# Head and tail of a fused S5 state-space and SwiGLU kernel: another order of the first four token tiles, and a last tile stored in three blocks

## The chip, the cores and the metric

The kernel runs on one core of a Trainium2 chip. The core has five engines with instruction streams of their own: TensorE (PE in the profile; its weight loads are PEld), VectorE (DVE), ScalarE (ACT), GpSimd (POOL) and SyncE (SP), which here only issues transfers. They meet through semaphores. Matmul results land in PSUM, 8 banks of 128 x 512 fp32; everything else is in SBUF. The metric is the time of one execution on the device, in microseconds, as the median of several runs.

## The reference

Input `x` is 2048 tokens of 512 features, bf16. It is normalised per token, and the normalised `xn` goes through two branches whose results are added to `x`:

```python
xn = (x - mean) / sqrt(var + 1e-5)
# A: diagonal complex state space, 512 states
Lam_bar = exp(exp(log_dt) * Lam)
Bu  = xn @ (((Lam_bar - 1) / Lam)[:, None] * B).T
h_t = Lam_bar * h_{t-1} + Bu_t
yA  = 2 * Re(h @ C.T) + xn * Dskip
# B: SwiGLU, hidden size 1376
yB  = (silu(xn @ w_gate) * (xn @ w_up)) @ w_down
out = x + yA + yB
```

## The kernel before

The 2048 tokens are 16 token tiles of 128 (`n`), four to a chunk of 512 (`c`). The hidden size is 11 feature tiles of 128 (`fi`), the last of 96. For a chunk and a feature tile TensorE makes gate and up (`gu_mm`, 4 matmuls each over the 512 features in four parts `k`) into two PSUM banks; ScalarE takes both out (Silu and copy), VectorE multiplies them. The B projection (`bproj_tile`) works likewise; VectorE rotates, scans and rotates back (`ssm_ops`). At the end of a chunk `out_ffn` and `out_ssm` add 11 + 8 matmuls per token tile into one bank.

Order is written out by hand: the kernel is under a manual schedule, so each engine executes its instructions as the Python program issues them. Long VectorE work stands in a backlog that `pump` lets out in step with the matmuls; none of it starts before the head ends. PSUM is a pool of 8 banks (`bank()`).

The **head** is the part up to the first 512-column matmul. `x` tiles 0 to 3 and the weights of feature tiles 0 to 3 come in first, over the queues of SP and ScalarE. Each of the four token tiles passes through
- `ln_stats` (VectorE: statistics, then an aggregate),
- `ln_rstd` (VectorE adds epsilon into `ve`, GpSimd raises it to -0.5),
- `norm_dve` (VectorE),
- `xT_pe` (four TensorE transposes into one bank, then one copy of 512 columns to `xnT`, by ScalarE, for tile 3 by VectorE).

Then `head_mm(fi, i)` runs gate and up of the first three feature tiles for that token tile alone: 8 matmuls of 128 columns into the banks `held`. Up to the first transposes TensorE runs dummy matmuls on a tile of zeros (`dummy`), and after them 11 short ones. The state-space parameters are transposed on TensorE too (`prm_transpose`, 12 columns), between token tiles 2 and 3, and go through ScalarE's Exp before its table for Silu is loaded. The order of the calls is:

```python
dummy(11, CW)
ln_stats(0); ln_rstd(0, 1); ln_stats(1); norm_dve(0); ln_rstd(1, 2)
xT_pe(0); dummy(11, 128)
ln_stats(2); norm_dve(1); ln_rstd(2, 3)
head_mm(0, 0); xT_pe(1); head_mm(1, 0); head_mm(2, 0)
```

The **tail** is the last token tile, 15. `out_blocks` cuts its 512 output columns in two blocks of 256; each has its own bank and matmuls, a VectorE addition of the residual and a store, the first on ScalarE's queue and the last on SP's.

Of the kernel before, what the change touches and what calls it, by code (L numbers as in the profile page):

```python
# [23 lines left out]
def kernel(  # L24
# [17 lines left out]
    nc = tc.nc  # L42
    _, L, D = A_x.shape
# [18 lines left out]
    EPS = 1e-5  # L62

    const = ctx.enter_context(tc.tile_pool(name="const", bufs=1))
# [8 lines left out]
    def bank(shape=(128, CW), dtype=F32):  # L73
        return psum.tile(list(shape), dtype, name="ps")
# [48 lines left out]
    prm_rows = const.tile([3 * NQ, 128], BF16, name="prm_rows")  # L123
# [28 lines left out]
    nc.vector.memset(junk[:], 0.0)  # L152
    neg_half = const.tile([128, TPC], F32, name="neg_half")
    nc.vector.memset(neg_half[:], -0.5)
    magic_t = const.tile([128, 1], F32, name="magic_t")
    nc.vector.memset(magic_t[:], MAGIC)
    ident = const.tile([128, 128], BF16, name="ident")
    make_identity(nc, ident[:])
    jidx = const.tile([128, CW], F32, name="jidx")
# [10 lines left out]
    def xn_tile(c):  # L170
        return xn_end if c == NCH - 1 else xall[:, c * TPC:(c + 1) * TPC, :]

    def ln_stats(n):
        nc.vector.bn_stats(out=stats[:, n, :], in_=xall[:, n, :])  # L174
        nc.vector.bn_aggr(out=mv[:, n, :], in_=stats[:, n, :])  # L175

    def ln_rstd(a, b):
        nc.vector.tensor_scalar(out=ve[:, a:b], in0=mv[:, a:b, 1], scalar1=EPS, scalar2=None, op0=ALU.add)  # L178
        nc.gpsimd.tensor_tensor(out=rstd[:, a:b], in0=ve[:, a:b], in1=neg_half[:, 0:b - a], op=ALU.pow)  # L179
# [5 lines left out]
    def norm_dve(n):  # L185
        c, i = divmod(n, TPC)
        nc.vector.tensor_scalar(out=xn_tile(c)[:, i, :], in0=xall[:, n, :], scalar1=mv[:, n, 0:1],  # L187
                                scalar2=rstd[:, n:n + 1], op0=ALU.subtract, op1=ALU.mult)
# [3 lines left out]
        nc.scalar.activation(out=xn_tile(c)[:, i, :], in_=xall[:, n, :], func=ACT.Identity,  # L192
                             scale=rstd[:, n:n + 1], bias=nb[:, n:n + 1])

    def xT_pe(n, on_dve=False):
        c, i = divmod(n, TPC)
        tp = bank((128, KD, 128), BF16)
        for k in range(KD):
            nc.tensor.transpose(out=tp[:, k, :], in_=xn_tile(c)[:, i, k * 128:(k + 1) * 128], identity=ident[:])  # L199
        if on_dve:  # L200
            nc.vector.tensor_copy(out=xnT[:, :, n * 128:(n + 1) * 128], in_=tp[:])
        else:
            nc.scalar.copy(out=xnT[:, :, n * 128:(n + 1) * 128], in_=tp[:])  # L203

    def xT_dma(n):
        c, i = divmod(n, TPC)
# [3 lines left out]
    prm = const.tile([128, 3, NQ], F32, name="prm")  # L210
# [8 lines left out]
    kk, fs1, fc1 = sm("kk", 2, NQ), sm("fs1", 2, NQ), sm("fc1", 2, NQ)  # L219
    V = nc.vector  # L220

    def prm_transpose():
        pp = bank((128, 3 * NQ), BF16)
        nc.tensor.transpose(out=pp[:], in_=prm_rows[:], identity=ident[0:3 * NQ, 0:3 * NQ])  # L224
        return pp

    def params_a(pp):
        V.tensor_copy(out=prm[:].rearrange("p t q -> p (t q)"), in_=pp[:])
        nc.scalar.activation(out=dt_t[:], in_=ldt, func=ACT.Exp)

    def params_a2():
        V.tensor_tensor(out=dre[:], in0=dt_t[:], in1=lre, op=ALU.mult)
        nc.scalar.activation(out=r_t[:], in_=dre[:], func=ACT.Exp)
        nc.scalar.preload_act_table_set("silu_and_others")
        V.scalar_tensor_tensor(out=ws2[:, 0, :], in0=dt_t[:], scalar=INV_2PI, in1=lim, op0=ALU.mult, op1=ALU.mult)
# [168 lines left out]
    def gu_mm(ps, groups, c, fi, lo, hi):  # L404
        fs = fsz[fi]
        for k in range(KD):
            nc.tensor.matmul(ps[:fs, lo:hi], lhsT=wslice(groups, fi, k),  # L407
                             rhs=xnT[:, k, c * CW + lo:c * CW + hi], start=(k == 0), stop=(k == KD - 1))
# [66 lines left out]

    def out_blocks(n):

        return ((0, D // 2), (D // 2, D)) if n == NT - 1 else ((0, D),)

    def out_ffn(n):  # L480
        c, i = divmod(n, TPC)
# [64 lines left out]

    GU = 8 * 0.2163
    BP = 4 * 0.2163
    warm = bank()

    def dummy(n, cols):
        for _ in range(n):
            nc.tensor.matmul(warm[:, 0:cols], lhsT=junk[:, 0:128], rhs=junk[:, 0:cols], start=True, stop=True)
# [15 lines left out]

    H = 3
    held = []

    def head_mm(fi, i):
        if len(held) <= fi:
            held.append((bank(), bank()))
        gu_mm(held[fi][0], wg_g, 0, fi, i * 128, (i + 1) * 128)
        gu_mm(held[fi][1], wu_g, 0, fi, i * 128, (i + 1) * 128)

    dummy(11, CW)
    ln_stats(0)
    ln_rstd(0, 1)
    ln_stats(1)
    norm_dve(0)
    ln_rstd(1, 2)
    xT_pe(0)
    dummy(11, 128)
    ln_stats(2)
    norm_dve(1)  # L590
    ln_rstd(2, 3)
    head_mm(0, 0)
    xT_pe(1)
    head_mm(1, 0)
    head_mm(2, 0)
    ln_stats(3)
    ln_rstd(3, 4)
    norm_dve(2)
    nc.gpsimd.iota(out=jidx[:], pattern=[[1, CW]], base=0, channel_multiplier=0,
                   allow_small_or_imprecise_dtypes=True)  # L600
    head_mm(0, 1)
    xT_pe(2)
    pp = prm_transpose()
    params_a(pp)
    head_mm(1, 1)
    head_mm(2, 1)
    norm_dve(3)
    params_a2()
    head_mm(0, 2)
    xT_pe(3, on_dve=True)  # L610
    head_mm(1, 2)
    head_mm(2, 2)
    params_sin()
    tables = table_ops()
    stats1, norm1 = ln_rest(1, False)
# [2 lines left out]
    queue("ln1", norm1)  # L618
    queue("tables", tables[2:])
    for fi in range(H):  # L620
        head_mm(fi, 3)
        gu_out(0, fi, *held[fi])
        pump(GU / 4)
    pump(2.0)
# [39 lines left out]
    G0 = 7  # L664
    for fi in range(H, G0):
        gateup_tile(0, fi)
# [77 lines left out]
```

## Time and profile before

| | us |
|---|---|
| median of 3 runs (lowest to highest) | 181.16 (181.07 to 181.38) |
| the profiled execution | 181.06 |
| its span, first to last instruction | 179.3 |
| TensorE busy | 174.4 (97%) |
| VectorE busy | 152.8 (85%) |
| ScalarE busy | 93.4 (52%) |
| GpSimd busy | 25.5 (14%) |

Times in the profile count from the start of the span. In a timeline row stand start, length, engine, line, operation, output and inputs, shapes and count; a bracket names the idle time before it and what ended that. A row with a count covers several instructions, from the start of the first to the end of the last. Groups by line give busy time and mean length in ns of one, then the idle time before them. DMA rows give the size and the time from issue to landing. Ends of matmuls are modelled, so a matmul's row is longer than the step to the next one.

### The profile page before, as it was taken

To read this page: it belongs to the slowest core of one execution; us is meant where nothing else is said; L and a number is where in the kernel's file an instruction comes from. 1 tells how busy PE (TensorE), PEld (TensorE's weight loads), DVE (VectorE), ACT (ScalarE), POOL (GpSimd) and SP (SyncE) were. 2 spreads that over 40 slices of the span, in tenths; PEclk is the share of its full clock that TensorE was granted. 3 is DMA by queue.
4 is the path that set the end of the run, shared out by engine and by line. 5 is a ranking of instruction groups with operands and counts; after the bars stand their busy time and mean duration, and the time that the engine had idled before them with its cause. 6 is when DMAs were issued, how large, how long until landed. Compare 5 with 4: busy or idle time off the path is not lost.

```text
span 179.3 us, 2445 instructions
## 1 busy us (share of the span) xinstructions
PE 174.4 (97%) x914; PEld 83.4 (47%) x914; DVE 152.8 (85%) x232; ACT 93.4 (52%) x165; POOL 25.5 (14%) x33
## 2 busy tenths in 40 slices
PE   7899999999999999999999999999999999999993
PEld 2694444444444444444444444444444444444642
DVE  2869997999999999999999999999999999940032
ACT  2279786988499867023998661024866610220000
POOL 5513000000500000028100000013405000150000
DMA  5999656994237500022920000007386900072011
GB/s 165 325 246 242 105 111 194 349 153 98 46 62 183 230 0 0 0 20 18 141 59 2 0 0 4 0 0 76 32 126 88 150 0 0 2 85 36 0 59 59
DMA packets 29371, 15.53 MB, mean 87 GB/s; under 512 B 18064, under 2 KB 29296, under 8 KB 29328
## 3 DMA queue, kind: packets, MB, share of 16 engines
q1 hardware_dynamic: 24416, 11.24, 27.2%
q0 software_dynamic: 3456, 3.28, 14.2%
q10 hardware_dynamic: 1488, 0.85, 1.6%
q8 instruction: 7, 0.11, 0.3%
q14 instruction: 4, 0.03, 0.0%
HBM read 8.03 MB, written 5.24 MB: 74 GB/s over the span
## 4 chain that ended last, share of the span: by engine, by line
PE 95%; DMA 1%; DVE 1%; ACT 0%; issue 0%
PE ps L407 39%; PE ps L487 21%; PE ps L496 15%; PE ps L332 15%; PE ps L433 2%; DMA xall<-in_A_x_dram 1%; PE ps L443 1%; DVE stats L174 1%; PE ps L199 1%; ACT xnT L203 0%; DVE res L499 0%; DVE mv L175 0%; DVE xall L187 0%; DVE ve L178 0%; PE ps L224 0%
## 5 line engine op out<-in xcount | busy, mean ns | idle before, releaser
L407 PE MATMUL ps<-xnT,wg 128*128 128x512 bf16 (+1 forms) x196 | 42.6, 340 | 0.1
L407 PE MATMUL ps<-xnT,wu 128*128 128x512 bf16 (+1 forms) x196 | 42.6, 340 | 0.0
L487 PE MATMUL ps<-wd_sb,guT 128*128 128x512 bf16 (+3 forms) x187 | 38.7, 366 | 0.0
L374 DVE TENSOR_TENSOR_SCAN g<-r_t,car,u 128x512 bf16<-128x512 f32 x24 | 28.9, 1267 | 0.0
L496 PE MATMUL ps<-CF,wt 128*128 128x512 bf16 (+1 forms) x136 | 28.3, 366 | 0.0
L332 PE MATMUL ps<-xnT,BT 128*128 128x512 bf16 x128 | 28.3, 379 | 0.0
L487 PEld LDWEIGHTS <-guT 128*128 128x128 bf16 (+1 forms) x187 | 18.3, 98 | 20.0
L502 ACT CAST res<-ps 128x512 bf16<-128x512 f32 x12 | 7.0, 585 | 38.6 <-PE ps L496 38.6
L421 ACT ACTIVATE guT<-ps 128x512 bf16<-128x512 f32 x40 | 24.7, 618 | 4.1 <-PE ps L407 4.0
L422 ACT CAST u<-ps 128x512 bf16<-128x512 f32 x40 | 24.1, 603 | 4.3 <-PE ps L407 4.0
L407 PEld LDWEIGHTS <-wu 128*128 128x128 bf16 x196 | 17.6, 98 | 17.5
L407 PEld LDWEIGHTS <-wg 128*128 128x128 bf16 x196 | 17.5, 98 | 17.8 <-issue 1.0
L503 POOL DMA_DIRECT2D out_dram<-res x12 | 11.1, 999 | 87.8 <-ACT res L502 87.8
L496 PEld LDWEIGHTS <-wt 128*128 128x128 bf16 x136 | 13.3, 98 | 14.4
L332 PEld LDWEIGHTS <-BT 128*128 128x128 bf16 x128 | 12.5, 98 | 15.1
L334 ACT CAST u<-ps 128x512 bf16<-128x512 f32 x32 | 17.6, 588 | 3.1 <-PE ps L332 3.1
L499 DVE TENSOR_TENSOR res<-ps,xn_end 128x512 bf16<-128x512 f32 (+1 forms) x5 | 2.9, 585 | 14.9 <-PE ps L496 14.9
L426 DVE TENSOR_TENSOR guT<-guT,u 128x1024 bf16<-128x1024 bf16 x20 | 13.5, 681 | 0.0
L179 POOL TENSOR_TENSOR rstd<-ve,neg_half 128x1 f32<-128x1 f32 (+1 forms) x7 | 7.6, 1082 | 39.0 <-DVE ve L178 39.0
L174 DVE BATCH_NORM_STATS2 stats<-xall 128x6 f32<-128x512 bf16 x16 | 10.8, 672 | 2.6 <-DMA xall<-in_A_x_dram 2.6
L342 DVE TENSOR_TENSOR pm<-u,c 128x2048 bf16<-128x2048 bf16 x8 | 9.8, 1221 | 1.2 <-ACT c L259 1.1
L342 DVE TENSOR_TENSOR pm<-g,c 128x2048 bf16<-128x2048 bf16 x8 | 9.8, 1219 | 0.1
(93 smaller groups left out, 141.4 us busy)
## 6 DMA issues: line engine op xcount, KB each, us to landing
out_dram<-in_A_x_dram SPq DMA_DIRECT2D x1, 1536.0 KB, 6.9
out_dram<-res POOLq DMA_DIRECT2D x12, 128.0 KB, 3.2
out_dram<-xall POOLq DMA_DIRECT2D x3, 512.0 KB, 6.4
wd_sb<-in_B_w_down_dram SPq DMA_DIRECT2D x1, 1280.0 KB, 11.1
xall<-in_A_x_dram SPq DMA_DIRECT2D x1, 1024.0 KB, 6.5
wg<-in_B_w_gate_dram SPq DMA_DIRECT2D x2, 384.0 KB, 5.6
wu<-in_B_w_up_dram SPq DMA_DIRECT2D x2, 384.0 KB, 5.3
wu<-in_B_w_up_dram ACTq DMA_DIRECT2D x2, 256.0 KB, 5.1
```

Source lines behind the costliest of these rows:

```text
L174: nc.vector.bn_stats(out=stats[:, n, :], in_=xall[:, n, :])
L332: nc.tensor.matmul(ps[:], lhsT=BT[:, part, k, q * 128:(q + 1) * 128], rhs=xnT[:, k, c * CW:(c + 1) * CW], start=(k == 0), stop=(k == KD - 1))
L334: nc.scalar.copy(out=u_tiles[c][:, part, q, :], in_=ps[:])
L342: V.tensor_tensor(out=t[:], in0=flat(src()[:, i]), in1=flat(tab[:]), op=ALU.mult)
L374: V.tensor_tensor_scan(out=g()[:, part, q, :], data0=r_t[:, q:q + 1].to_broadcast([128, CW]), data1=u_tiles[c][:, part, q, :], initial=ini ...
L407: nc.tensor.matmul(ps[:fs, lo:hi], lhsT=wslice(groups, fi, k), rhs=xnT[:, k, c * CW + lo:c * CW + hi], start=(k == 0), stop=(k == KD - 1))
L421: nc.scalar.activation(out=guT[:fs, fi, :], in_=psg[:fs], func=ACT.Silu)
L422: nc.scalar.copy(out=u_pair[c][:fs, fi % 2, :], in_=psu[:fs])
L426: products.append(lambda: V.tensor_tensor(out=g, in0=g, in1=u, op=ALU.mult))
L487: nc.tensor.matmul(o[:], lhsT=gu_tiles[c][:fsz[fi], fi, i * 128:(i + 1) * 128], rhs=wd_sb[:fsz[fi], fi, lo:hi], start=(fi == 0), stop=False)
L496: nc.tensor.matmul(o[:], lhsT=w_tiles[c][:, part, q, i * 128:(i + 1) * 128], rhs=CF[:, part, q, lo:hi], start=False, stop=(part == 1 and q ...
L503: nc.gpsimd.dma_start(out=out_v[:, n, lo:hi], in_=res[:, lo:hi], accum_op=ALU.add)
```

## The change

In the head:
- ScalarE makes the `rstd` of token tile 0 (`rstd_act`: Ln with epsilon as bias, then Exp with scale -0.5) from a table set that holds both and is loaded ahead; tiles 1 to 3 keep `ln_rstd`.
- `xT_pe` puts two transposes into a bank and copies 256 columns, twice for a token tile; `head_mm` can run over half of `k`, and for tile 0 and tile 1 the first half's matmuls of two feature tiles stand ahead of the second half's.
- VectorE's order: tile 0 is normalised ahead of tile 1's aggregate, tile 1 ahead of tile 2's statistics, tile 2 between tile 3's statistics and its aggregate, tile 3 ahead of the parameters' copy.
- Feature tile 2 runs for token tiles 0 and 1 at once, with 256 columns, after tile 1's other matmuls.
- The parameter transpose shares a bank with token tile 2's second half.
- There are 10 wide dummies and 6 short ones.

In the tail the last token tile has blocks of 256, 128 and 128 columns, the first two stored from ScalarE's queue and the last from SP's.

```diff
-    magic_t = const.tile([128, 1], F32, name="magic_t")
-    nc.vector.memset(magic_t[:], MAGIC)
+    eps_t = const.tile([128, 1], F32, name="eps_t")
+    nc.vector.memset(eps_t[:], EPS)
...
+    def rstd_act(n):
+
+        nc.scalar.activation(out=ve[:, n:n + 1], in_=mv[:, n, 1:2], func=ACT.Ln, bias=eps_t[:, 0:1])
+        nc.scalar.activation(out=rstd[:, n:n + 1], in_=ve[:, n:n + 1], func=ACT.Exp, scale=-0.5)
...
-    def xT_pe(n, on_dve=False):
+    def xT_pe(n, parts, on_dve=False, prm_too=False):
+
         c, i = divmod(n, TPC)
-        tp = bank((128, KD, 128), BF16)
-        for k in range(KD):
-            nc.tensor.transpose(out=tp[:, k, :], in_=xn_tile(c)[:, i, k * 128:(k + 1) * 128], identity=ident[:])
-        if on_dve:
-            nc.vector.tensor_copy(out=xnT[:, :, n * 128:(n + 1) * 128], in_=tp[:])
-        else:
-            nc.scalar.copy(out=xnT[:, :, n * 128:(n + 1) * 128], in_=tp[:])
+        kp = KD // parts
+        for k0 in range(0, KD, kp):
+            tp = bank((128, kp * 128 + 3 * NQ), BF16)
+            for k in range(k0, k0 + kp):
+                nc.tensor.transpose(out=tp[:, (k - k0) * 128:(k - k0 + 1) * 128],
+                                    in_=xn_tile(c)[:, i, k * 128:(k + 1) * 128], identity=ident[:])
+            if prm_too and k0 + kp == KD:
+                prm_transpose(tp[:, kp * 128:])
+            dst, src = xnT[:, k0:k0 + kp, n * 128:(n + 1) * 128], tp[:, 0:kp * 128].rearrange("p (k t) -> p k t", k=kp)
+            if on_dve:
+                nc.vector.tensor_copy(out=dst, in_=src)
+            else:
+                nc.scalar.copy(out=dst, in_=src)
+        return tp[:, kp * 128:]
...
-        return ((0, D // 2), (D // 2, D)) if n == NT - 1 else ((0, D),)
+        return ((0, D // 2), (D // 2, D - 128), (D - 128, D)) if n == NT - 1 else ((0, D),)
...
-    warm = bank()
+    H = 3
+    held = [(bank(), bank()) for _ in range(H)]
+    warm = held[0][0]
...
+    def head_mm(which, lo, hi, ks, fis):
+
+        for fi in fis:
+            for k in ks:
+                nc.tensor.matmul(held[fi][which][:, lo * 128:hi * 128], lhsT=wslice((wg_g, wu_g)[which], fi, k),
+                                 rhs=xnT[:, k, lo * 128:hi * 128], start=(k == 0), stop=(k == KD - 1))
+
+    allk = range(KD)
+    nc.scalar.preload_act_table_set("natural_log_exp_and_others")
+    dummy(10, CW)
     ln_stats(0)
-    ln_rstd(0, 1)
-    ln_stats(1)
+    rstd_act(0)
+    nc.vector.bn_stats(out=stats[:, 1, :], in_=xall[:, 1, :])
     norm_dve(0)
+    nc.vector.bn_aggr(out=mv[:, 1, :], in_=stats[:, 1, :])
     ln_rstd(1, 2)
-    xT_pe(0)
-    dummy(11, 128)
+    xT_pe(0, 2)
+    dummy(6, 128)
+    norm_dve(1)
     ln_stats(2)
-    norm_dve(1)
     ln_rstd(2, 3)
-    head_mm(0, 0)
-    xT_pe(1)
-    head_mm(1, 0)
-    head_mm(2, 0)
-    ln_stats(3)
+
+    head_mm(0, 0, 1, range(0, HK), (0, 1))
+    head_mm(0, 0, 1, range(HK, KD), (0, 1))
+    head_mm(1, 0, 1, allk, (0,))
+    xT_pe(1, 2)
+    head_mm(1, 0, 1, allk, (1,))
+    nc.vector.bn_stats(out=stats[:, 3, :], in_=xall[:, 3, :])
+    norm_dve(2)
+    nc.vector.bn_aggr(out=mv[:, 3, :], in_=stats[:, 3, :])
     ln_rstd(3, 4)
-    norm_dve(2)
...
-    head_mm(0, 1)
-    xT_pe(2)
-    pp = prm_transpose()
-    params_a(pp)
-    head_mm(1, 1)
-    head_mm(2, 1)
-    norm_dve(3)
+    head_mm(0, 1, 2, range(0, HK), (0, 1))
+    head_mm(0, 1, 2, range(HK, KD), (0, 1))
+    head_mm(1, 1, 2, allk, (0, 1))
+    head_mm(0, 0, 2, allk, (2,))
+    pp = xT_pe(2, 2, prm_too=True)
+    head_mm(1, 0, 2, allk, (2,))
+    norm_dve(3)
+    params_a(pp)
     params_a2()
-    head_mm(0, 2)
-    xT_pe(3, on_dve=True)
-    head_mm(1, 2)
-    head_mm(2, 2)
+    head_mm(0, 2, 3, range(0, HK), range(H))
+    head_mm(0, 2, 3, range(HK, KD), range(H))
+    head_mm(1, 2, 3, allk, (0,))
+    xT_pe(3, 2, on_dve=True)
+    head_mm(1, 2, 3, allk, (1, 2))
...
     for fi in range(H):
-        head_mm(fi, 3)
+        head_mm(0, 3, 4, allk, (fi,))
+        head_mm(1, 3, 4, allk, (fi,))
         gu_out(0, fi, *held[fi])
```

More of the change, by code (lines that the diff above doesn't have):

```diff
@@ L220, with prm_transpose @@
     V = nc.vector
[L222 to L225, printed above, removed]
+    def prm_transpose(pp):
+        nc.tensor.transpose(out=pp, in_=prm_rows[:], identity=ident[0:3 * NQ, 0:3 * NQ])
     def params_a(pp):
-        V.tensor_copy(out=prm[:].rearrange("p t q -> p (t q)"), in_=pp[:])
+        V.tensor_copy(out=prm[:].rearrange("p t q -> p (t q)"), in_=pp)
         nc.scalar.activation(out=dt_t[:], in_=ldt, func=ACT.Exp)
@@ L568, in ln_rest @@
         return ops, tail
[L572 to L581, printed above, removed]
+    HK = KD // 2
+    def head_mm(which, lo, hi, ks, fis):
[6 more added lines that the diff above has]
+    dummy(10, CW)
     ln_stats(0)
-    ln_rstd(0, 1)
-    ln_stats(1)
+    rstd_act(0)
+    nc.vector.bn_stats(out=stats[:, 1, :], in_=xall[:, 1, :])
     norm_dve(0)
+    nc.vector.bn_aggr(out=mv[:, 1, :], in_=stats[:, 1, :])
     ln_rstd(1, 2)
-    xT_pe(0)
-    dummy(11, 128)
+    xT_pe(0, 2)
+    dummy(6, 128)
+    norm_dve(1)
     ln_stats(2)
-    norm_dve(1)
     ln_rstd(2, 3)
-    head_mm(0, 0)
-    xT_pe(1)
-    head_mm(1, 0)
-    head_mm(2, 0)
-    ln_stats(3)
+    head_mm(0, 0, 1, range(0, HK), (0, 1))
[6 more added lines that the diff above has]
+    nc.vector.bn_aggr(out=mv[:, 3, :], in_=stats[:, 3, :])
     ln_rstd(3, 4)
-    norm_dve(2)
     nc.gpsimd.iota(out=jidx[:], pattern=[[1, CW]], base=0, channel_multiplier=0,
                    allow_small_or_imprecise_dtypes=True)
-    head_mm(0, 1)
-    xT_pe(2)
-    pp = prm_transpose()
+    head_mm(0, 1, 2, range(0, HK), (0, 1))
[5 more added lines that the diff above has]
+    norm_dve(3)
     params_a(pp)
-    head_mm(1, 1)
-    head_mm(2, 1)
-    norm_dve(3)
     params_a2()
-    head_mm(0, 2)
-    xT_pe(3, on_dve=True)
-    head_mm(1, 2)
-    head_mm(2, 2)
+    head_mm(0, 2, 3, range(0, HK), range(H))
[3 more added lines that the diff above has]
+    head_mm(1, 2, 3, allk, (1, 2))
     params_sin()
```

## The prediction

> **What bounds the kernel now.** I read the page first, its busy times and its chain of waits, then the timeline of each engine for the first 14 us and the last 5 us, which are the only places that the change touches.
>
> ```profile
> PE 174.4 (97%) x914; PEld 83.4 (47%) x914; DVE 152.8 (85%) x232; ACT 93.4 (52%) x165; POOL 25.5 (14%) x33
> ...
> PE 95%; DMA 1%; DVE 1%; ACT 0%; issue 0%
> ```
>
> TensorE is the bound: 95% of the chain. What is left is the time before its first useful matmul, a few stalls among the short matmuls of the head, and the tail behind its last one. The change can win or lose only there. TensorE, head and start of the wide matmuls:
>
> ```profile
> 1.20 3.95 PE L553 MATMUL ps<-junk 128*128 128x512 bf16 x11 [1.20 <-DVE magic_t L156]
> ...
> 5.72 0.40 PE L199 MATMUL ps<-ident,xall 128*128 128x128 bf16 x4 [0.58 <-DVE ve L178]
> 5.96 0.78 PE L553 MATMUL ps<-junk 128*128 128x128 bf16 x11
> 6.79 0.38 PE L407 MATMUL ps<-xnT,wg 128*128 128x128 bf16 x4
> ...
> 8.93 0.39 PE L199 MATMUL ps<-ident,xall 128*128 128x128 bf16 x4
> 9.25 0.18 PE L224 MATMUL ps<-ident,prm_rows 12*128 12x12 bf16 x1
> 9.36 0.23 PE L407 MATMUL ps<-xnT,wg 128*128 128x128 bf16 x1
> ...
> 13.17 0.38 PE L407 MATMUL ps<-xnT,wg 128*128 128x512 bf16 x1
> ```
>
> A 128-column matmul takes 0.056 us in a stream ((0.78 - 0.22)/10, where 0.22 is the modelled end of the last; a lone one ends 0.22 after its start, so four transposes end 0.39 to 0.40 after theirs). From 6.79 to 13.17 there are 96 head matmuls, 12 transposes and one parameter transpose: 109 x 0.056 = 6.10 of 6.38 us, so 0.28 us is stall. Of this 0.15 lies around the parameter transpose (8.93 + 4 x 0.056 = 9.15, it starts at 9.25, and the next at 9.36 rather than 9.31). The predicted quantity of the head is the start of the first wide matmul, now 13.17: behind it TensorE runs as a stream.
>
> The chain before the first matmul, VectorE, then GpSimd, then ScalarE:
>
> ```profile
> 4.18 0.18 DVE L175 BATCH_NORM_AGGREGATE mv<-stats 128x2 f32<-128x6 f32 x1
> 4.40 0.15 DVE L178 TENSOR_SCALAR ve<-mv 128x1 f32<-128x1 f32 x1
> 4.47 0.68 DVE L174 BATCH_NORM_STATS2 stats<-xall 128x6 f32<-128x512 bf16 x1
> 5.18 0.18 DVE L175 BATCH_NORM_AGGREGATE mv<-stats 128x2 f32<-128x6 f32 x1
> 5.28 0.38 DVE L187 TENSOR_SCALAR xall<-xall,mv,rstd 128x512 bf16<-128x512 bf16 x1
> ```
> ```profile
> 4.63 0.58 POOL L179 TENSOR_TENSOR rstd<-ve,neg_half 128x1 f32<-128x1 f32 x1 [1.00 <-DVE ve L178]
> ```
> ```profile
> 6.16 0.58 ACT L203 COPY xnT<-ps 128x512 bf16<-128x512 bf16 x1 [2.10 <-PE ps L199]
> ...
> 9.84 0.21 ACT L229 ACTIVATE dt_t<-prm 128x4 f32<-128x4 f32 x1
> 10.28 0.21 ACT L233 ACTIVATE r_t<-dre 128x4 f32<-128x4 f32 x1 [0.23 <-DVE dre L232]
> 10.50 1.28 ACT L234 ACT_TABLE_LOAD   x1
> ...
> 12.68 0.58 ACT L421 ACTIVATE guT<-ps 128x512 bf16<-128x512 f32 x1
> ```
>
> The reader is to see the hand-overs: an independent VectorE instruction begins 0.08 before the end of the last (5.28 against 5.18 + 0.18), ScalarE likewise 0.10 (9.84 against 9.36 + 0.58), GpSimd 0.08 after VectorE, the transposes 0.06 after the normalised tile (5.66 to 5.72), the copy 0.04 after the transposes, the matmul 0.05 after the copy. The first normalisation at 5.28 starts when the second tile's aggregate is all but over, not when GpSimd's power ends at 5.21.
>
> **The change, part by part.**
>
> *rstd of tile 0 on ScalarE.* Removed from the chain: `ve` 0.15 on VectorE and the power 0.58 on GpSimd. Added: Ln and Exp on [128,1]. Nothing in the trace is a Ln; the nearest rows are the two ScalarE ACTIVATEs at 0.21, and the Ln has a pointer bias, whose price is bounded by these groups (one pointer and two):
>
> ```profile
> L315 ACT ACTIVATE cm<-CT,c2re 128x512 f32<-128x512 bf16 x4 | 2.9, 726 | 0.1
> L192 ACT ACTIVATE xn_end<-xall,nb,rstd 128x512 bf16<-128x512 bf16 x4 | 3.2, 812 | 1.8 <-DVE nb L182 1.7
> ```
>
> So the Ln takes 0.21 to 0.31; I take 0.31, since it has the pointer and these groups lie 0.09 apart; were the bias free, the sum would be 0.1 lower. Ln 4.40 to 4.71, Exp 4.74 to 4.95, normalisation from 4.98. VectorE does not stop that: without `ve`, tile 1's statistics run from 4.28 to 4.96, and the aggregate of tile 1 now stands behind the normalisation. So the normalised tile is ready at 5.36, was 5.66. The constant `eps_t` takes the place of `magic_t`, one memset for another. The built program has one table load ahead of the Ln where the old one had one ahead of the first copy, so none is added.
>
> *Copies in halves.* A copy of 256 columns is in no row. Between 0.21 at 4 columns and 0.58 at 512 the line gives 0.39; the lower bound is half of 0.58, the upper 0.58. I take 0.39, nearest to both rows. Transposes from 5.42; the second ends at 5.70; first half copied 5.74 to 6.13, second 6.03 to 6.42. First matmul at 6.18 (was 6.79), its four run out at 6.40, and the other half lets it on at 6.47: 0.07 of stall. The six short dummies end their issue at 5.98, ahead of 6.18. Eight more matmuls: 6.92.
>
> *Tile 1 ahead of tile 2's statistics.* Aggregate 5.28 to 5.46, `ve` to 5.65, power 5.73 to 6.31, normalisation 6.36 to 6.74, transposable at 6.80, before TensorE comes at 6.92. VectorE idles meanwhile, and tile 2 is late for it: statistics to 7.34, power to 8.37, tile 3's statistics beside it, normalised at 8.83.
>
> *Feature tile 2 for two token tiles, and the stalls of the new order.* After tile 1's transposes (from 6.92) only four matmuls cover the half copy, which is usable 0.06 + 0.22 + 0.04 + 0.39 + 0.05 = 0.76 after the first transpose: TensorE is idle from 7.36 to 7.67, 0.31, and 0.06 at the second half. Then 12 short ones to 8.62, and feature tile 2 for both token tiles. Its weights:
>
> ```profile
> 2.20 0.43 SPq L112 DMA_DIRECT2D wg<-in_B_w_gate_dram  x1
> 2.29 0.46 ACTq L112 DMA_DIRECT2D wu<-in_B_w_up_dram  x1
> ...
> wg<-in_B_w_gate_dram SPq DMA_DIRECT2D x1, 256.0 KB, 5.6
> ...
> wu<-in_B_w_up_dram ACTq DMA_DIRECT2D x1, 256.0 KB, 5.9
> ```
>
> They land at 7.8 and 8.2; used before at about 8.0 and 8.25 and now at 8.62 and later, so this move takes the transfers off the path. Eight matmuls of 256 columns at 0.109 (tail, below) against 16 of 0.056: 0.02 saved. Tile 2's transposes at 9.06 find it ready; its copies are covered by 0.44 of wide matmul and the parameter transpose, whose 0.15 stays. Tile 3's copies are on VectorE:
>
> ```profile
> 9.47 0.17 DVE L228 CAST prm<-ps 128x12 f32<-128x12 bf16 x1 [0.82 <-PE ps L224]
> ...
> 11.13 0.42 DVE L201 COPY xnT<-ps 128x512 bf16<-128x512 bf16 x1 [0.82 <-PE ps L199]
> ```
>
> By the same line a half is 0.29 (bounds 0.21 and 0.42); transposes at 10.81, eight matmuls as cover, 0.07 of stall at the second half. Sum: first matmul 6.18; work 80 x 0.056 + 8 x 0.109 + 13 x 0.056 = 6.08; stalls 0.07 + 0.31 + 0.06 + 0.15 + 0.07 = 0.66; first wide matmul at 12.92 with these rounded prices, against 6.79 + 6.10 + 0.28 = 13.17 before. **Head: -0.25.** Started 0.61 earlier, it gives 0.38 back in stalls, and 0.02 is less work. SP's queue is not touched here; ScalarE's table load for Silu moves from 10.50 to about 10.9 and ends at 12.2, and the first Silu stays near 12.68. GpSimd's iota is wanted only by the tables, after the chunk's statistics. TensorE coming 0.25 us earlier to the wide matmuls meets nothing late there: the first Silu frees its bank at 13.26, and the second wide pair asks for it near 12.92 + 8 x 0.216 = 14.6 (a wide one by twice 0.109, rounded).
>
> *Last tile 256+128+128.*
>
> ```profile
> 174.41 1.80 PE L496 MATMUL ps<-CF,wt 128*128 128x256 bf16 x15
> ...
> 175.43 0.42 DVE L499 TENSOR_TENSOR res<-ps,xn_end 128x256 bf16<-128x256 f32 x1 [0.18 <-PE ps L496]
> 176.25 0.42 DVE L499 TENSOR_TENSOR res<-ps,xn_end 128x256 bf16<-128x256 f32 x1 [0.39 <-PE ps L496]
> 176.70 0.33 SPq L500 DMA_DIRECT2D out_dram<-res  x1
> ...
> 174.56 0.69 DVE L499 TENSOR_TENSOR res<-ps,xn_end 128x512 bf16<-128x512 f32 x1 [1.09 <-PE ps L496]
> ...
> L739 SPq EVENT_SEMAPHORE  x7: 27/28/28, 177.1 to 177.5; - x7
> ```
>
> A 256-column matmul takes (1.80 - 0.27)/14 = 0.109; 19 of them (11 FFN, 8 SSM) become 38 of 0.056: +0.05. The last addition falls from 0.42: 0.69 at 512 and 0.42 at 256 give 0.29 at 128, -0.13; its neighbour's is over before. The closing waits on SP follow in a fixed order of semaphores, 0.07 apart; the built program now has the last store's wait last, where one followed it: -0.07 (bounds -0.1 and 0). The store itself:
>
> ```profile
> out_dram<-res SPq DMA_DIRECT2D x3, 128.0 KB, 1.7
> ...
> out_dram<-res SPq DMA_DIRECT2D x1, 64.0 KB, 1.5
> w_last<-in_B_w_gate_dram SPq DMA_DIRECT2D x1, 64.0 KB, 2.4
> ```
>
> 128 KB to 64 KB saved 0.2, rows halved from 1024 to 512 bytes; 32 KB with 256-byte rows is bounded by 1.4 and by the 2.4 of a transfer in 128-byte rows. I take 1.5, the nearest row, so 0. The Trainium skill, "DMA: Bandwidth & Descriptors", Specifications, speaks against this: it has full rate only from 512 bytes a row and a read-modify-write below. By the rows the sum stands as below; by that rule the store is dearer and the sum is that of the slow-store rival. No run here stores so small a row. The second 128 columns leave on ScalarE's queue behind the first store's 0.35 of issue, at about 176.4, ahead of SP's 176.6. **Tail: +0.05 - 0.13 - 0.07 = -0.15.**
>
> **Sum.** -0.25 - 0.15 = -0.40 on the profiled execution of 181.06 (span 179.3): 180.66. The median shown, 181.16, is 0.10 above that execution; against it the forecast is 180.76, -0.22%. About 0.2%, 0.36 us, is what a measurement of this kernel can tell from no change.
>
> **Rivals.**
> - *The head gives back what it gains; the same time.* Four half copies stand on the path (two of tile 0, two of tile 1). If each costs 0.45 instead of 0.39, the head is -0.01 and the sum -0.16: 181.0. For it: no row has a half copy. Against: VectorE's addition fell from 0.69 to 0.42 when halved. Below 0.42 per copy the time is nearer to the forecast.
> - *The small store at the end is slow; slower.* Place: the last SP store, 256 bytes a row. At the 2.4 us of the 128-byte rows the tail is +0.75 and the sum +0.50: 181.66. It decides from about 2.3 us. Against: halving the row from 1024 to 512 bytes made the store faster, and the 2.4 was among other traffic.
> - *TensorE loses its rate; slower.* The dummies' weight loads are 0.42 apart until this point and 0.22 then:
>
> ```profile
> 3.73 0.15 PEld L553 LDWEIGHTS <-junk 128*128 128x128 bf16 x1 [0.28 <-issue]
> 4.12 0.32 PEld L553 LDWEIGHTS <-junk 128*128 128x128 bf16 x2 [0.23 <-issue]
> ```
>
>   One wide and five short dummies less, and stalls of 0.31: if the slow rate comes back for 2.9 us, as long as it lasted (1.20 to 4.1), 1.45 us is lost: 182.2. Against: 0.57 us idle before 5.72 cost nothing here. It decides from 0.8 us of lost work. The Trainium skill, "TensorE: Matmul & The Clock Gate", The HAM clock gate, takes the rate back only after an idle window of some 3.4 us; by that rule this rival does not happen, and the trace agrees as far as its 0.57 goes.
> - *Cheaper than taken; faster still.* Ln 0.21 and half copies of 0.36: another 0.10 + 0.12, 180.54.
>
> **How the numbers follow.** Forecast with the cheaper case 0.60, given back 0.26, slow store 0.08, lost rate 0.06. The first holds 180.5 to 180.9, its upper edge inside the 0.2%, so a tenth of the whole goes from it to no change; the second lies within 0.2% but for a little. Faster 0.54, same 0.32, slower 0.14. For eight in ten: 180.45, under the cheaper case, to 181.25, over the given-back one with the closing waits and 0.2 us of the store against it.
>
> **What would show it.** Right: normalised tile 0 near 5.4, first useful matmul near 6.2, an idle stretch of about 0.3 near 7.4 released by ScalarE's copy, first wide matmul near 12.9, the last addition near 0.29, the store near 1.5. Wrong: half copies over 0.45, a wait of TensorE on tile 1's normalisation, short matmuls 0.11 apart, a store over 2 us, or a TensorE stall after the head that was not there.

## The result, and the profile after

The changed kernel takes 180.58 us (median of 9 runs, 180.34 to 180.83), the kernel before beside it 181.22 us (median of 9, 181.07 to 181.89). The ratio is 0.9958, 95% interval 0.9948 to 0.9968: 0.6 to 0.9 us faster. The forecast was 180.76, 0.40 us faster, in a range from 180.45 to 181.25 that holds the result.

The two profiled executions stand nearer to each other than the runs: 180.64 (span 178.9) against 181.06 (179.3), 0.42 us. That difference between 0.42 and 0.6 to 0.9 is the question of this case.

The head of the changed kernel, TensorE's timeline from 0 to 13.4 us:

```profile
1.19 3.63 PE L566 MATMUL ps<-junk 128*128 128x512 bf16 x10 [1.19 <-DVE eps_t L156]
5.52 0.40 PE L207 MATMUL ps<-ident,xall 128*128 128x128 bf16 x4 [0.70 <-DVE xall L192]
5.76 0.50 PE L566 MATMUL ps<-junk 128*128 128x128 bf16 x6
6.27 0.66 PE L591 MATMUL ps<-xnT,wg 128*128 128x128 bf16 x8
6.76 0.39 PE L591 MATMUL ps<-xnT,wu 128*128 128x128 bf16 x4
6.99 0.39 PE L207 MATMUL ps<-ident,xall 128*128 128x128 bf16 x4
7.21 0.39 PE L591 MATMUL ps<-xnT,wu 128*128 128x128 bf16 x4
7.72 0.66 PE L591 MATMUL ps<-xnT,wg 128*128 128x128 bf16 x8
...
9.10 0.39 PE L207 MATMUL ps<-ident,xall 128*128 128x128 bf16 x4
9.42 0.18 PE L236 MATMUL ps<-ident,prm_rows 12*128 12x12 bf16 x1
9.53 0.61 PE L591 MATMUL ps<-xnT,wu 128*128 128x256 bf16 x4
...
12.95 0.81 PE L418 MATMUL ps<-xnT,wg 128*128 128x512 bf16 x3
```

The first useful matmul starts at 6.27 (before 6.79), the first wide one at 12.95 (13.17). The holes stand where the forecast put them: 7.21 + 4 x 0.056 = 7.43, and the next starts at 7.72; 9.10 + 4 x 0.056 = 9.32, then 9.42 and 9.53.

The work ahead of the first transposes, and the half copies, from the timelines of ScalarE and VectorE:

```profile
4.49 0.29 ACT L179 ACTIVATE ve<-mv,eps_t 128x1 f32<-128x1 f32 x1 [0.43 <-DVE mv L175]
4.81 0.20 ACT L180 ACTIVATE rstd<-ve 128x1 f32<-128x1 f32 x1
...
5.84 0.65 ACT L215 COPY xnT<-ps 128x256 bf16<-128x256 bf16 x2 [0.83 <-PE ps L207]
```
```profile
5.05 0.41 DVE L192 TENSOR_SCALAR xall<-xall,mv,rstd 128x512 bf16<-128x512 bf16 x1
```

ScalarE's half copies average 0.375 in groups by form, VectorE's 0.287. The tail, from 174 us, and its stores:

```profile
175.24 0.68 DVE L510 TENSOR_TENSOR res<-ps,xn_end 128x256 bf16<-128x256 f32 x2 [0.18 <-PE ps L507]
175.70 0.89 ACTq L511 DMA_DIRECT2D out_dram<-res  x2
176.08 0.29 DVE L510 TENSOR_TENSOR res<-ps,xn_end 128x128 bf16<-128x128 f32 x1 [0.15 <-PE ps L507]
```
```profile
out_dram<-res ACTq DMA_DIRECT2D x1, 32.0 KB, 1.6
out_dram<-res SPq DMA_DIRECT2D x1, 32.0 KB, 1.5
```

The last addition is 0.29 instead of 0.42, and the store of 256-byte rows lands as fast as the 512-byte one did.

From the first wide matmul to the end of the span it is 166.13 us in the kernel before and 165.92 here. These two figures come back in every trace below: 166.13 with two blocks, 165.91 to 165.93 with three. So in the traces the tail is worth 0.21, and all else is in the start of the first wide matmul. A profiled run's time lies 1.76 to 1.80 us above the end of its span in all fourteen traces, so a time also tells about where its first wide matmul was.

### The profile page after: what moved, and what is told of

Its sections match the earlier page's. It is cut to its first block, busy times and chain, and to the rows that moved or that the text cites. A ratio compares the mean times of both kernels' runs of the same rounds, so it can differ in the third digit from the quotient of the medians.

```text
span 178.9 us, 2463 instructions
## 1 busy us (share of the span) xinstructions
PE 174.0 (97%) x919; PEld 83.5 (47%) x919; DVE 153.2 (86%) x233; ACT 93.8 (52%) x170; POOL 24.9 (14%) x32
## 4 chain that ended last, share of the span: by engine, by line
PE 95%; DMA 2%; DVE 1%; ACT 0%; issue 0%
PE ps L418 36%; PE ps L498 21%; PE ps L507 15%; PE ps L343 15%; PE ps L591 3%; PE ps L444 2%; DMA xall<-in_A_x_dram 2%; PE ps L454 1%; PE ps L207 1%; DVE stats L174 0%; DVE stats L599 0%; DVE xall L192 0%; ACT xnT L215 0%; PE ps L566 0%; DVE res L510 0%
## 5 line engine op out<-in xcount | busy, mean ns | idle before, releaser
L418 PE MATMUL ps<-xnT,wg 128*128 128x512 bf16 x148 | 38.0, 379 | 0.0
L418 PE MATMUL ps<-xnT,wu 128*128 128x512 bf16 x148 | 38.0, 379 | 0.0
L507 PE MATMUL ps<-CF,wt 128*128 128x512 bf16 (+2 forms) x144 | 28.3, 355 | 0.0
L418 PEld LDWEIGHTS <-wu 128*128 128x128 bf16 x148 | 14.5, 98 | 17.4
L418 PEld LDWEIGHTS <-wg 128*128 128x128 bf16 x148 | 14.3, 98 | 17.6 <-issue 0.8
L507 PEld LDWEIGHTS <-wt 128*128 128x128 bf16 x144 | 13.4, 98 | 14.3
L510 DVE TENSOR_TENSOR res<-ps,xn_end 128x512 bf16<-128x512 f32 (+2 forms) x6 | 3.0, 514 | 14.4 <-PE ps L507 14.4
L437 DVE TENSOR_TENSOR guT<-guT,u 128x1024 bf16<-128x1024 bf16 x20 | 13.6, 682 | 0.0
L184 POOL TENSOR_TENSOR rstd<-ve,neg_half 128x1 f32<-128x1 f32 (+1 forms) x6 | 6.9, 1154 | 40.2 <-DVE ve L183 40.2
L174 DVE BATCH_NORM_STATS2 stats<-xall 128x6 f32<-128x512 bf16 x14 | 9.4, 670 | 2.4 <-DMA xall<-in_A_x_dram 2.4
```

The source lines that it names most:

```text
L437: products.append(lambda: V.tensor_tensor(out=g, in0=g, in1=u, op=ALU.mult))
L507: nc.tensor.matmul(o[:], lhsT=w_tiles[c][:, part, q, i * 128:(i + 1) * 128], rhs=CF[:, part, q, lo:hi], start=False, stop=(part == 1 and q ...
```

## Experiments

The kernel before was run beside each group, each other kernel 5 to 12 times. Ratios are to the kernel before, with a 95% interval. "First wide" is the start of the first 512-column matmul in the profiled execution.

| kernel | median us | ratio | first wide |
|---|---|---|---|
| tail alone | 181.28 | 0.9984 (0.9971 to 0.9998) | 13.43 |
| head alone | 181.01 | 0.9969 (0.9955 to 0.9982) | 12.96 |
| fewer dummies alone | 181.52 | 0.9999 (0.9985 to 1.0013) | 13.53 |
| changed, whole copies | 181.59 | 0.9999 (0.9986 to 1.0012) | 13.83 |
| changed, old VectorE order | 181.02 | 0.9970 (0.9958 to 0.9982) | 13.85 |
| changed, feature tile 2 per token tile | 181.64 | 0.9998 (0.9983 to 1.0012) | 14.22 |
| changed, `rstd` by GpSimd | 180.81 | 0.9953 (0.9938 to 0.9967) | 13.13 |
| changed, tile 0's copies on VectorE | 180.64 | 0.9947 (0.9933 to 0.9961) | 12.85 |
| changed, again | 180.64 | 0.9955 (0.9939 to 0.9970) | 12.92 |
| changed, `rstd` by GpSimd, again | 180.77 | 0.9959 (0.9945 to 0.9973) | 13.07 |
| changed, padded parameter transpose | 180.42 | 0.9942 (0.9928 to 0.9956) | 12.78 |
| changed, more of the same | 180.39 | 0.9937 (0.9921 to 0.9953) | 12.73 |

The first four ran together, with the kernel before at 181.54; the next four on another chip, beside 181.65; the last four on the first chip again, beside 181.51. The changed kernel itself was not run on the other chip, so there only the ratios compare with it.

### Tail alone, head alone

The kernel before with the new tail:

```diff
-        return ((0, D // 2), (D // 2, D)) if n == NT - 1 else ((0, D),)
+        return ((0, D // 2), (D // 2, D - 128), (D - 128, D)) if n == NT - 1 else ((0, D),)
```

> The kernel before with the last tile in blocks of 256, 128 and 128 columns and nothing else. If the parts add up, the tail is worth what the two traces show behind the first wide matmul: +0.05 of TensorE, -0.13 in the last addition, -0.12 from there to the end, so about -0.20 us. Rival: the extra matmuls and the extra store eat it up, 0 to +0.1. A slow store of 256-byte rows would show as more than 2 us from issue to landing, against 1.5.

The changed kernel with the old tail, the same edit the other way:

> The changed kernel with the last tile in two blocks as before, so the head alone. If the parts add up: first wide matmul near 12.95 as in the changed kernel, and about -0.45 us in the medians, the rest of the -0.64. Rival: the head is worth what the pair of profiles shows, -0.22, and the excess of the medians is scatter.

Measured: the tail 0.3 us (0.04 to 0.5), the head 0.56 us (0.33 to 0.8); together 0.85 against 0.76 for the whole, so the two parts add up within their intervals. The head is worth more than the 0.25 of the forecast. The traces of the old head show where that can come from. This is the chain of waits of the tail-alone kernel, whose head is the old one (start, length, what):

```profile
1.65 4.49 DMA xall<-in_A_x_dram
6.14 0.02 issue
6.17 0.70 DVE stats L174
6.87 0.02 issue
6.90 0.18 DVE mv L175
7.08 0.30 DVE xall L187
7.38 0.07 DVE ve L178
7.45 0.38 PE ps L199 x4
```

Against it the same stretch of the chain of the profiled execution before, on which the forecast was made:

```profile
0.74 2.69 DMA xall<-in_A_x_dram
3.43 0.02 issue
3.45 0.70 DVE stats L174
```

In the execution that was shown, the chain begins at `x` tile 0, landed at 3.43. In this one, with the same code, it begins at `x` tile 2, landed at 6.14: VectorE takes tile 2's statistics first, and tile 1's normalisation stands behind them. TensorE waits for tile 1 from 7.28 to 7.43. But this is not its last wait. TensorE's timeline goes on, and the view of the line of these matmuls names what ended their idle time:

```profile
7.89 0.39 PE L407 MATMUL ps<-xnT,wu 128*128 128x128 bf16 x4
8.29 0.40 PE L407 MATMUL ps<-xnT,wg 128*128 128x128 bf16 x4
...
13.43 1.03 PE L407 MATMUL ps<-xnT,wg 128*128 128x512 bf16 x4
```
```profile
  DMA wg<-in_B_w_gate_dram: 0.2, 1
```

TensorE is free at 7.89 + 4 x 0.056 = 8.11 and starts feature tile 2 at 8.29, when its gate weights have landed (8.25). An earlier `x` tile 2 would only have made that wait longer. The chain of waits leaves it out, because the modelled end of the matmul before, 8.28, covers it. The three traces of the old head compare like this (us; waits of TensorE, landings in brackets):

| trace | first useful | wait for tile 1 (`x` tile 2) | wait for feature tile 2's weights (gate, up) | first wide |
|---|---|---|---|---|
| before | 6.79 | 0.08 (6.03) | 0.03 (7.82, 8.21) | 13.17 |
| tail alone | 6.84 | 0.15 (6.14) | 0.18 (8.25, 8.41) | 13.43 |
| fewer dummies | 6.97 | 0.21 (6.33) | 0.09 (8.28, 8.57) | 13.53 |

In all three the weights end the last wait that depends on a transfer: from the first up matmul of feature tile 2 (8.25, 8.53, 8.62) to the first wide matmul it is 4.90 to 4.92. The execution that was shown had both transfers early, and its 181.06 us is at the lower end of the nine runs beside the changed kernel (181.07 to 181.89).

### Fewer dummies alone

```diff
-    dummy(11, CW)
+    dummy(10, CW)
...
-    dummy(11, 128)
+    dummy(6, 128)
```

> The kernel before with 10 wide and 6 short dummies in place of 11 and 11. By the forecast the dummies end ahead of the normalised tile in both, so 0 and the same 13.17. Rival: in some executions TensorE comes to its full rate later, the 11 wide dummies (0.43 each at the slow rate, 4.7 us) then run past the normalised tile at 5.7 and delay it by up to 0.2; then this kernel is 0.1 to 0.2 us faster in the medians, with less scatter.

No difference. Its trace is the third row of the table above: its chain of waits begins at `x` tile 2 too (6.33), TensorE waits longest for tile 1, then for both weights of feature tile 2, and the first wide matmul is at 13.53.

### Whole copies

```diff
-    xT_pe(0, 2)
+    xT_pe(0, 1)
...
-    xT_pe(1, 2)
+    xT_pe(1, 1)
...
-    pp = xT_pe(2, 2, prm_too=True)
+    pp = xT_pe(2, 1, prm_too=True)
...
-    xT_pe(3, 2, on_dve=True)
+    xT_pe(3, 1, on_dve=True)
```

> The changed kernel with one copy of 512 columns per token tile. If the half copies carry the head: first matmul 0.32 later (6.59), a stall of 0.6 behind tile 1's transposes instead of 0.3, and stalls of 0.1 to 0.3 at tiles 2 and 3: first wide matmul near 13.85, +0.9 us on the changed kernel and about +0.25 on the one before. Rival: the copies are mostly covered and the early rstd carries the head: +0.1 to +0.3 on the changed kernel.

Everything that the change gained is gone, about 0.75 us. TensorE's timeline shows the places:

```profile
6.48 0.61 PE L591 MATMUL ps<-xnT,wg 128*128 128x128 bf16 x8 [0.34 <-ACT xnT L215]
...
8.21 0.61 PE L591 MATMUL ps<-xnT,wg 128*128 128x128 bf16 x8 [0.45 <-ACT xnT L215]
```

The new order has only four matmuls between tile 1's transposes and their use, where the old one had sixteen. It can afford that with half copies only.

### The old VectorE order

The changed kernel with tile 2's statistics ahead of tile 1's normalisation again:

```diff
-    norm_dve(1)
     ln_stats(2)
+    norm_dve(1)
     ln_rstd(2, 3)
```

> The changed kernel with one step put back: VectorE takes the statistics of token tile 2 ahead of the normalisation of token tile 1, as the kernel before does. Theory now held (the old order waits for a transfer that scatters): the x rows of tile 2 landed at 5.77 to 6.33 us in the six executions profiled so far, 6.13 in the middle; the normalisation of tile 1 would end at about 7.36 instead of 6.85, tile 1's transposes wait for it, and the whole is 0.25 to 0.5 us slower than the changed kernel, so about 0.3 us faster than the kernel before (ratio about 0.998). In its trace TensorE has a hole of about 0.4 us ahead of tile 1's transposes, and the hole is as late as the landing of x tile 2. Rival (the prediction as recorded, which costed this step at nothing): 0 to 0.05 us slower than the changed kernel, ratio about 0.996.

It is 0.2 to 0.4 us slower than the changed kernel (ratio 0.9970 against 0.9955 to 0.9958; medians 181.02 against 180.58 and 180.64). That is nearer to the theory than to the 0 to 0.05 of the forecast, but the intervals of the ratios overlap and the two kernels ran on different chips. The trace carries it further than the times. VectorE, then GpSimd, then TensorE:

```profile
6.61 0.69 DVE L174 BATCH_NORM_STATS2 stats<-xall 128x6 f32<-128x512 bf16 x1 [0.94 <-DMA xall<-in_A_x_dram]
...
7.44 0.38 DVE L192 TENSOR_SCALAR xall<-xall,mv,rstd 128x512 bf16<-128x512 bf16 x1
```
```profile
5.76 0.58 POOL L184 TENSOR_TENSOR rstd<-ve,neg_half 128x1 f32<-128x1 f32 x1 [2.15 <-DVE ve L183]
```
```profile
6.69 0.39 PE L591 MATMUL ps<-xnT,wu 128*128 128x128 bf16 x4
7.88 0.40 PE L207 MATMUL ps<-ident,xall 128*128 128x128 bf16 x4 [0.80 <-DVE ve L183]
```

VectorE sits idle for 0.94 us until `x` tile 2 lands. Tile 1's `rstd` is there from 6.34, so only about the last 0.25 us of this keeps tile 1 waiting; then tile 2's statistics and aggregate stand ahead of it for another 0.83. Its normalisation starts at 7.44, where the changed kernel's second trace, with the same `rstd` at nearly the same time, has it at 6.38. TensorE then has a hole of about 1 us (6.69 + 4 x 0.056 = 6.91 to 7.88). This profiled execution was the slowest of the kernel's twelve (181.54), so the hole is not the usual one; it shows what the order does when the transfer is late. Feature tile 2's weights no longer stand behind the hole, so here it goes into the first wide matmul (13.85, against 12.92 in the changed kernel's second trace).

### Feature tile 2 for each token tile

```diff
     head_mm(1, 0, 1, allk, (1,))
+    head_mm(0, 0, 1, allk, (2,))
+    head_mm(1, 0, 1, allk, (2,))
...
-    head_mm(0, 0, 2, allk, (2,))
+    head_mm(0, 1, 2, allk, (2,))
...
-    head_mm(1, 0, 2, allk, (2,))
+    head_mm(1, 1, 2, allk, (2,))
```

> The changed kernel with feature tile 2 multiplied for token tile 0 and for token tile 1 separately, for tile 0 right behind feature tile 1, which is the place it had before. Theory (weights land late): TensorE comes to feature tile 2 at about 7.43, its gate weights land at 8.04 to 8.28 and its up weights at 8.36 to 8.57 in the executions profiled so far, so the eight multiplications end at 8.65 to 8.8 instead of tile 1 starting at 7.72; of these 0.95 to 1.05 us, 0.43 comes back since only four narrow rather than wide ones each are left behind tile 1: about 0.5 us slower than the changed kernel (0.45 to 0.65), ratio to the kernel before about 0.9985. Rival (weights are no limit, the eight multiplications of 0.056 us only fill the 0.29 us in which TensorE waits for tile 1's first half copy): 0.25 to 0.29 us faster than the changed kernel, ratio about 0.9945.

It loses 0.7 to 0.8 us against the changed kernel by the ratios, a little more than the theory's upper end; the rival is out. The times are those of the kernel before again: 180.95 to 182.09 here, 181.11 to 182.31 there. TensorE's timeline:

```profile
7.22 0.39 PE L591 MATMUL ps<-xnT,wu 128*128 128x128 bf16 x4
8.12 0.40 PE L591 MATMUL ps<-xnT,wg 128*128 128x128 bf16 x4 [0.51 <-DMA wg<-in_B_w_gate_dram]
9.16 0.40 PE L591 MATMUL ps<-xnT,wu 128*128 128x128 bf16 x4 [0.65 <-DMA wu<-in_B_w_up_dram]
```

The up weights landed at 9.12, where the expectation had counted on 8.57 at the latest. The four traces from this chip have them at 9.12 to 9.51, the ten others of this case at 8.21 to 9.02. The changed kernel asks for them at 9.53, on that chip with nothing to spare: in the trace there with tile 0's copies on VectorE they landed at 9.39, and the up matmuls start at 9.43, 0.23 behind the parameter transpose instead of 0.11.

### `rstd` of tile 0 by GpSimd, twice

```diff
-    rstd_act(0)
+    ln_rstd(0, 1)
```

> The changed kernel with the reciprocal deviation of token tile 0 by VectorE and GpSimd as before, all else changed. Theory (the head is one chain from x tile 0): normalised tile 0 comes about 0.3 us later, first useful multiplication at about 6.57 instead of 6.27, and nothing behind absorbs it, so 0.3 us slower than the changed kernel (0.25 to 0.4), ratio to the kernel before about 0.9975. Rival (later waits, for weights or for tile 1, absorb it): 0 to 0.1 us slower, ratio about 0.996.

> The reciprocal deviation of token tile 0 by VectorE and GpSimd again, now beside the changed kernel itself. Where it was measured alone, its ratio to the kernel before was 0.9953, no worse than that of the changed kernel elsewhere. In that trace x tile 0 landed at 3.17 and the up weights of feature tiles 0 and 1 only at 6.89, behind the first useful multiplication at 6.20. Theory (the chain from x tile 0 sets the head): 0.25 to 0.3 us slower than the changed kernel beside it. Rival (the landing of the first up weights, 6.4 to 6.9 us in the four traces of that session against 5.45 to 5.74 in the six before, sets the head, and an earlier first multiplication only waits there): 0 to 0.1 us slower; its trace then shows the first up multiplications starting at the landing of their weights.

In the traces the theory holds: from the landing of `x` tile 0 to the first useful matmul it is 3.03 us in both (3.17 to 6.20, 3.36 to 6.39), against 2.75 to 2.78 with ScalarE, 0.25 to 0.28 more. In the times it does not show: the medians beside each other are 180.77 and 180.64, the ratios 0.9959 and 0.9955. The two profiled executions behind these last two differ by 0.15 (180.77, 180.62), with `x` tile 0 landed 0.10 earlier in the one with GpSimd, which makes up the 0.25. What absorbed the first trace was the rival's transfer (the up weights, on the chain of waits until 6.89; TensorE's up matmuls begin at 6.94). In the second nothing absorbed it. So this step saves 0.25 to 0.28 us of the chain, and between 0 and that in the time; the runs do not settle where.

### The changed kernel again

> The changed kernel itself once more, so that the next kernels have it beside them under the same conditions. In its trace the first wide multiplication is looked at again: theory now held (the new head hangs on x tile 0 and hardly on the landing of x tile 2): 9.4 us behind the landing of x tile 0, as in the two profiled executions of this head so far (9.42 and 9.42), whatever the landing of x tile 2 is, as long as the gate and up weights of feature tiles 0 and 1 have landed by then. Rival (the new head scatters as the old one): 9.6 us or more. Ratio to the kernel before 0.9958 as first measured, within 0.001.

First wide 9.46 us behind `x` tile 0 (3.46 to 12.92), with `x` tile 2 landed at 6.55, and 9.42 in the two other traces of this head, with 5.77 and 6.16: the landing of `x` tile 2 has lost its hold.

The chain of this trace has a new beginning:

```profile
1.19 4.45 PE ps L566 x10
5.64 0.25 PE ps L207 x4
```

The ten dummies took 4.45 us here and 3.63 in the changed kernel's first trace, since TensorE's rate rose later. The chain puts them, not `x`, before the transposes, but it goes by their modelled end, 5.64; the transposes start at 5.46, 0.06 behind the normalised tile as in the first trace. The dummies were just out of the way; only the transposes ran a little slower (0.43 instead of 0.40).

### Shorter still

Tile 0's half copies on VectorE:

```diff
-    xT_pe(0, 2)
+    xT_pe(0, 2, on_dve=True)
```

> The changed kernel with the two half copies of token tile 0 on VectorE instead of ScalarE. Theory (each half copy of tile 0 stands on the chain): VectorE's half copy took 0.28 to 0.29 us where ScalarE's took 0.37, so the first useful multiplication starts at about 6.19 instead of 6.27 and the whole is 0.08 us faster (0.03 to 0.1), ratio to the kernel before about 0.9955. Rival (VectorE then comes too late to the normalisation of tile 1, which stands behind the copies): 0 to 0.1 us slower.

From `x` tile 0 to the first useful matmul 2.67 instead of 2.75, the 0.08 expected; in the time (0.9947 against 0.9955 to 0.9958) it is no more than a hint. The first wide matmul comes 9.53 behind `x` tile 0, not earlier than 9.42: in this trace the up weights of feature tile 2 came late, as told above.

The parameter rows padded with zeros:

```diff
-    prm_rows = const.tile([3 * NQ, 128], BF16, name="prm_rows")
+    prm_rows = const.tile([128, 128], BF16, name="prm_rows")
+    nc.gpsimd.memset(prm_rows[:], 0.0)
...
-        nc.tensor.transpose(out=pp, in_=prm_rows[:], identity=ident[0:3 * NQ, 0:3 * NQ])
+        nc.tensor.transpose(out=pp, in_=prm_rows[:], identity=ident[:])
```

> The changed kernel with the transpose of the 12 parameter rows padded with zeros to 128 rows. Theory (the short weight load of 12 rows costs TensorE the 0.15 us hole seen around it, from 9.27 to 9.42 and 9.53): the hole goes, one multiplication of 0.056 us stays, 0.1 us faster than the changed kernel. Rival (the hole is the wait for the parameter rows or for a bank, not the short load): 0 us.

The hole is gone; the steps are 0.22 and 0.06 where they were 0.32 and 0.11:

```profile
9.08 0.39 PE L208 MATMUL ps<-ident,xall 128*128 128x128 bf16 x4
9.30 0.22 PE L237 MATMUL ps<-ident,prm_rows 128*128 128x128 bf16 x1
9.36 0.60 PE L592 MATMUL ps<-xnT,wu 128*128 128x256 bf16 x4
```

The weight loads of this transpose, in the changed kernel and here, where the transpose before starts at 9.27 and 9.25:

```profile
9.41 0.09 PEld L236 LDWEIGHTS <-prm_rows 12*128 12x128 bf16 x1
```
```profile
9.25 0.10 PEld L237 LDWEIGHTS <-prm_rows 128*128 128x128 bf16 x1
```

The load of 12 rows starts 0.15 behind the start of the transpose before it, the load of 128 rows together with it. The rows had landed by 7.36 and 7.67, and the bank is the one that the transposes before just filled, so the rival is out. The 0.10 ahead of the short load is the load's, since it comes before its matmul; the 0.05 behind may be the load's or that of the matmul of 12 columns, which the padding changed too.

The first wide matmul is 0.14 earlier than in the changed kernel beside it, the median 0.22, more than the 0.1 expected. The last kernel puts this and the copies on VectorE together with two more steps:

```diff
-    ln_rstd(1, 2)
-    xT_pe(0, 2)
+    rstd_act(1)
+    xT_pe(0, 2, on_dve=True)
...
-    ln_rstd(2, 3)
...
-    head_mm(1, 0, 1, allk, (0,))
+    head_mm(1, 0, 1, range(0, HK), (0,))
     xT_pe(1, 2)
+    rstd_act(2)
+    head_mm(1, 0, 1, range(HK, KD), (0,))
```

> The changed kernel with more of the same: the half copies of token tile 0 on VectorE (0.08 us), the padded parameter transpose (0.1 us), the reciprocal deviations of token tiles 1 and 2 also on ScalarE, and tile 1's transposes two up multiplications earlier, so that six multiplications instead of four cover the first half copy of tile 1 (0.29 us of waiting becomes about 0.1). Theory (the head is one chain of short steps, each worth its time): 0.35 us faster than the changed kernel (0.2 to 0.45), ratio to the kernel before about 0.994. Rival (transfers set the head from here on): no faster than the changed kernel, within 0.1 us.

It is 0.25 us faster than the changed kernel by the medians (180.39 against 180.64), inside the theory's range but no better than the padding alone can be shown to be (180.42). Its trace says why: tile 0 was normalised at 5.26, and TensorE was not there.

```profile
1.19 4.45 PE L567 MATMUL ps<-junk 128*128 128x512 bf16 x10 [1.19 <-DVE eps_t L157]
5.44 0.63 PE L208 MATMUL ps<-ident,xall 128*128 128x128 bf16 x4
```

The last dummy held it to 5.44, 0.12 later than the usual 0.06 behind the tile, and the transposes ran at the low rate, 0.63 instead of 0.40. Fewer dummies could win back that 0.12, not what the low rate costs; that was not tried.

## Why the prediction was right, and where it was not

The direction and the range were right, and the terms of the sum hold against the execution that was profiled: 0.40 forecast, 0.42 between the two traces. That the range held the median too is in part luck: in the runs the head gained about twice what was forecast, and the range ended only 0.13 below the result.

- *`rstd` on ScalarE.* Ln 0.31 forecast, 0.29; Exp 0.21 and 0.20. The normalisation takes 0.41 instead of 0.38. With `x` tile 0 landing 0.09 later, tile 0 is ready at 5.46 instead of 5.36. From the landing to the first useful matmul 0.61 was to be saved, and it was (3.36 to 2.75).
- *Half copies.* 0.39 forecast, 0.375; VectorE 0.29 and 0.287. The given-back rival, which needed 0.45, falls.
- *Stalls of the new order.* 0.66 forecast, 0.62 found: 0.05 at tile 0's second half (0.07), 0.29 and 0.05 at tile 1 (0.31 and 0.06), 0.15 at the parameter transpose (0.15), 0.07 at tile 3 (0.07).
- *Head.* 13.17 to 12.95, 0.22 against 0.25 forecast; counted from the landing of `x` tile 0 it is 0.31.
- *Tail.* 0.15 forecast, 0.21: the addition -0.13 as said, the matmuls +0.05 as said, the closing waits -0.09 instead of -0.07, the store -0.03 instead of 0. The slow-store rival falls: 1.5 us, not 2.4. The Trainium skill, "DMA: Bandwidth & Descriptors", Specifications, has full rate only from 512 bytes and a read-modify-write below. The trace shows no price of it for this store (1.50, against 1.53 with 512-byte rows and twice the bytes).
- *TensorE's rate.* No short matmul behind tile 0's transposes runs at the low rate in the changed kernel, and fewer dummies alone cost nothing (0.9999). The lost-rate rival falls.
- *Cheaper than taken.* This rival's time, 180.54, is the nearest to the median, but not by its mechanism: the Ln took 0.29 and not 0.21, the half copies 0.375 and not 0.36.

What was mis-sized is the head in the runs, 0.25 where they show about 0.55 (0.76 less the tail's 0.21; 0.56 for the head alone). The new head came out as summed. The step that failed is the old head beside it: "0.28 us is stall" was read off one execution and set into the sum as if it were fixed, and the move of feature tile 2, which "takes the transfers off the path", was thereby priced at 0.02 of work and the 0.03 of waiting that this one execution shows. By the same sum the stalls are 0.49 and 0.46 in the other two traces of the old head (13.43 - 6.84 - 6.10, 13.53 - 6.97 - 6.10). What differs are the waits for tile 1, behind `x` tile 2, and for feature tile 2's weights, and the weights end the last of them.

How much that is in the usual execution can be estimated. In the ten traces that are not from the other chip, most of them of changed kernels, the up weights of feature tile 2 land at 8.43 in the middle; with 0.05 to their first matmul and 4.92 from there the old head's first wide matmul comes to 13.4, where the new head is at 12.92 to 12.96: 0.45 instead of 0.22, and with the tail about 0.66, between the profiled pair's 0.42 and the 0.76 of the ratio. The medians of the kernel before say 13.3 (181.22) and, in the later groups, 13.6 to 13.8 (181.51 to 181.65); its slower runs were not profiled, so whether the weights land later still in them stays open. So does the split between the two moves: no run has the old head with one of them alone. In the new head, the weights put back cost 0.7 to 0.8, all of the gain, and the old VectorE order 0.2 to 0.4.

The parts are no sum. Whole copies lose 0.75, feature tile 2 per token tile 0.75, the old VectorE order 0.2 to 0.4, together far more than the head's 0.55: each of these steps makes the others necessary or possible. In the old head an earlier tile 1 would have met the wait for the weights; only with the weights out of the way does VectorE's order count in full.

## What to carry to other kernels

One profiled execution shows one draw of the transfers. Before its stalls go into a sum as fixed, and before a reordering is costed at nothing, ask which landing each stall waits for, and what it costs if that landing is 0.3 us later. Where two waits follow each other on one engine, the later one decides, and the chain of waits can miss it: check the starts of the instructions against the landings. A dummy loop ahead of the first real work is a floor of its own: its length has to be judged at the low rate.

## What the runs showed of the hardware

- The same transfer, issued at 1.65 in the chains shown, lands at 5.77 to 6.71 us from one execution to the next. The second transfer of up weights came at 9.12 to 9.51 in the four traces from one chip and at 8.21 to 9.02 in the others.
- TensorE's rate rose between 2.5 and 2.9 us behind the first dummy in four of the fourteen traces, where the step from dummy to dummy falls from 0.43 to 0.22. In the last kernel's trace it rose only at 5.0 us, where short dummies were still 0.11 apart up to 6.18 and 0.056 from 6.25. So ten dummies took 3.63 us in one execution and 4.45 in another. The Trainium skill, "TensorE: Matmul & The Clock Gate", The HAM clock gate, puts the rise about 4 us into sustained work, half a microsecond more or less; these traces scatter more.
- A weight load of 12 rows (the parameter transpose) starts only 0.15 us behind the start of the transpose before it, where a load of 128 rows starts together with it. With the matmul of 12 columns it costs TensorE about 0.15 us of waiting in all.
